# A spectral layer and a gated feed-forward on one core: the scheduler's other timing model

## The chip, the cores and the metric

One core of a Trainium2 chip runs the whole program. The metric is the device time of one execution in microseconds (us). The kernel before took 2654.95, 2657.49 and 2660.61 us in three runs; the median is 2657.49 us.

Five engines work side by side, each through its own instructions in a fixed order: PE (TensorE, matmuls; its weight loads are shown apart as PEld), DVE (VectorE), ACT (ScalarE), POOL (GpSimd) and SP (SyncE), which here issues the DMAs. An instruction that has to wait holds up everything behind it on its engine.

## The reference

For each of 8 batches, x has 3008 rows of 256 columns. The first half is a filter in the frequency domain, the second a feed-forward with a gate over all 24064 rows:

```python
X = np.fft.rfft(x, axis=1)
Yr = Xr @ w_r - Xi @ w_i + b_r          # Yi likewise
Y  = shrink(Yr, 0.01) + 1j * shrink(Yi, 0.01)
y  = np.fft.irfft(Y, n=3008, axis=1)
h  = y.reshape(24064, 256) @ w_in       # 256 x 2048
g  = h * np.clip(h + 3.0, 0.0, 6.0) / 6.0
out = g @ w_out                         # 2048 x 256
```

`shrink` moves each value towards 0 by 0.01 and stops at 0. `w_in` and `w_out` come in double precision.

## The kernel before

**The filter.** 3008 is 64 times 47, so each transform is done as two short ones, by matmuls with constant tables. Per batch there are three stages with DRAM scratch between them. `stage1` (line 496) loads x (`xin`), adds and subtracts mirrored halves (lines 520 and 521, on POOL from batch 2 on), multiplies by the 47-point table and stores `a`. `middle` (line 595) loads `bt`, does the 64-point transform (`s2`), the products with the weights and the shrinking (`s3`; `X` and `tc` are its tiles), and the way back (`s4`, `s5`). `segment` (line 697) loads `qt` and makes the rows of y in `raw`, a tile of 512 rows.

**The feed-forward.** The 24064 rows are 47 chunks of 512, and the 2048 inner columns 8 blocks of 256, so there are 376 units. `prepare` (line 793) makes seven operands `yb` of a chunk from `raw` by sums and differences, since the product with `w_in` is done by a scheme of seven half-size products in place of eight. A unit goes through `phase_a` to `phase_d` (lines 829 to 856): matmuls add up in the PSUM tiles `pb`, `pc` and `pd`; between them ACT copies an intermediate sum out of `pb` (`p`, `u`; line 824, and `h`, line 855) and DVE adds it to `pc` or `pd` into `h` (line 827). The next product that adds up in `pc` has to wait for that DVE add. There are two buffers of `pb`, and one each of `pc` and `pd`. `gate` (line 858) makes `r` and then `gs` of `h`: ACT line 862, DVE line 864, ACT line 131, DVE line 132. `down` (line 869) multiplies `gs` by `w_out` into `po`, in four calls a unit.

**Precision.** Each operand is split into a high and a low part (`split`, line 129), and `product` (line 134) does three matmuls where one would do: low by high, high by low, high by high. The three are called a triple below.

**The order in the code.** One loop (line 974) writes the units down as in a pipeline: in turn i stand `phase_a` of unit i, `phase_c`, `phase_d` and the start of the gate of unit i-1, `phase_b` of unit i, the rest of the gate of unit i-2, and the four `down` calls of unit i-3, one between each two phases. The stages of the filter are generators that are laid into quarter-turn slots (`lay`, line 920): a segment, for one, begins 8.5 units before its first row is used.

**The order that runs.** The framework's scheduler does not keep the order of the code. When the `TileContext` (line 1036) closes, it plays the program against a timing model of the machine: when an engine can take an instruction, it gets the one that stands first in the code among those whose inputs and buffers the model counts as there. What comes out is a fixed list of instructions for each engine, with the semaphores that it needs. Two helpers add edges by hand: `in_order` (line 174) ties every instruction of the start (the first batch's filter up to the first two chunks' operands) to the one before it on its engine, and `behind` (line 186) puts the last pieces of weight preparation after that start. From the first unit on, nothing else is tied.

## Time and profile before

| | |
|---|---|
| time, median of three | 2657.49 us |
| profiled execution, its own time | 2661.04 us |
| span of that execution in the trace | 2659.2 us |
| PE busy | 2586.7 us (97%), 16502 matmuls |
| DVE busy | 1962.6 us (74%) |
| ACT busy | 1816.4 us (68%) |
| POOL busy | 770.2 us (29%) |
| mean granted TensorE clock | 0.990 |

Busy time is the time in which an engine has an instruction in work; matmuls overlap, so that their steps (from start to start) are shorter than their durations.

### The profile page before, as it was taken

The page shows a single profiled execution, that of the slowest core. Times are in us where ns is not written, and L with a number is a line of the kernel's source. Part 1 is how long each engine was busy: PE and PEld are TensorE (multiplying, and loading weights), DVE is VectorE, ACT ScalarE, POOL GpSimd, SP SyncE. Part 2 cuts the span into 40 slices and gives each one's busy share as a digit, 9 for nine tenths or more (in the row PEclk, how much of TensorE's full clock was granted, in tenths as well). Part 3 has the DMA queues.
Part 4 walks back from the last instruction along what each step waited for, and adds up shares of the span by engine and source line. Part 5 has one row for each costly group of instructions (what it writes and reads, how often), then busy time and mean ns, then how long its engine had stood idle before and what let it go on. Part 6 is the DMA issues. An engine that isn't in the chain of part 4 may idle for free.

```text
span 2659.2 us, 44438 instructions
## 1 busy us (share of the span) xinstructions
PE 2586.7 (97%) x16502; PEld 2312.8 (87%) x16502; DVE 1962.6 (74%) x3175; ACT 1816.4 (68%) x3578; POOL 770.2 (29%) x739
## 2 busy tenths in 40 slices
PE   8789999999999999999999999999999999999999
PEld 5678889888888888888998988898899999999987
DVE  5877867777777777777777777777777777766666
ACT  3566767666766676676776777677676667666766
POOL 2253333332322332323323333323321122121210
PEclk9899999999999999999999999999999999999999
DMA  7524432222122221232212222222212111100000
GB/s 224 161 78 115 135 98 73 82 87 68 56 82 80 78 71 52 81 94 73 73 55 87 81 80 62 77 75 72 85 55 66 58 53 57 40 25 30 19 17 16
DMA packets 146096, 197.46 MB, mean 74 GB/s; under 512 B 16224, under 2 KB 101080, under 8 KB 145880
## 3 DMA queue, kind: packets, MB, share of 16 engines
q1 hardware_dynamic: 145879, 194.64, 25.0%
q8 instruction: 129, 2.11, 0.3%
q14 instruction: 88, 0.71, 0.1%
HBM read 97.58 MB, written 74.97 MB: 65 GB/s over the span
## 4 chain that ended last, share of the span: by engine, by line
PE 65%; DVE 10%; ACT 7%; issue 3%; POOL 1%; DMA 1%; ACTq 0%; SPq 0%; DVEq 0%; POOLq 0%
PE po L138 28%; PE pb L138 14%; PE pc L138 8%; PE ps_a L138 8%; PE pd L138 4%; ACT r L862 3%; DVE r L864 3%; PE ps_a L725 2%; DVE gs L132 2%; ACT gs L131 2%; PE ps_a L614 2%; DVE h L827 1%; DVE X L132 1%; DVE tc L655 1%; DMA xin<-in_x 0%
## 5 line engine op out<-in xcount | busy, mean ns | idle before, releaser
L138 PE MATMUL po<-gs,w_out_hi 128*128 128x512 f32 x3008 | 951.4, 397 | 1.8 <-DVE gs L132 1.8
L864 DVE SCALAR_TENSOR_TENSOR r<-r,h 128x1024 f32<-128x1024 f32 x376 | 478.0, 1271 | 381.8 <-ACT r L862 381.6
L138 PEld LDWEIGHTS po<-gs,w_out_hi 128*128 128x128 f32 x3008 | 565.7, 189 | 75.0 <-DVE gs L132 3.5
L138 PE MATMUL po<-gs,w_out_lo 128*128 128x512 f32 x1504 | 608.3, 405 | 2.3 <-ACT gs L131 2.3
L138 PE MATMUL pb<-yb,w_in_hi 128*128 128x256 f32 x3008 | 601.8, 282 | 0.0
L132 DVE TENSOR_TENSOR gs<-r,gs 128x1024 fp32r<-128x1024 f32 x376 | 476.4, 1267 | 124.8 <-ACT gs L131 122.0
L862 ACT ACTIVATE r<-h,three 128x1024 f32<-128x1024 f32 x376 | 433.3, 1152 | 192.5 <-DVE h L827 189.7
L138 PEld LDWEIGHTS pb<-yb,w_in_hi 128*128 128x128 f32 x3008 | 464.1, 190 | 50.4
L131 ACT CAST gs<-r 128x1024 fp32r<-128x1024 f32 x376 | 395.9, 1053 | 135.6 <-DVE r L864 122.7
L132 POOL TENSOR_TENSOR yb<-T,yb 128x256 fp32r<-128x256 f32 x184 | 204.9, 1124 | 815.1 <-ACT yb L131 815.0
L138 PE MATMUL pb<-yb,w_in_lo 128*128 128x256 f32 x1504 | 426.9, 284 | 8.8 <-ACT h L855 5.6
L827 DVE TENSOR_TENSOR h<-pc,u 128x256 f32<-128x256 f32 x752 | 313.9, 417 | 64.6 <-PE pc L138 60.5
L824 ACT COPY u<-pb 128x256 f32<-128x256 f32 x752 | 276.8, 371 | 104.0 <-PE pb L138 96.2
L138 PEld LDWEIGHTS pb<-yb,w_in_lo 128*128 128x128 f32 x1504 | 284.6, 189 | 67.3 <-ACT h L855 6.8
L138 PE MATMUL pc<-yb,w_in_hi 128*128 128x256 f32 x1504 | 299.6, 280 | 0.0
L138 PEld LDWEIGHTS po<-gs,w_out_lo 128*128 128x128 f32 x1504 | 284.1, 189 | 11.8 <-ACT gs L131 1.8
L138 PE MATMUL pc<-yb,w_in_lo 128*128 128x256 f32 x752 | 217.3, 289 | 23.3 <-DVE h L827 22.5
L855 ACT COPY h<-pb 128x256 f32<-128x256 f32 x376 | 140.0, 372 | 140.4 <-PE pb L138 139.1
L138 PEld LDWEIGHTS pc<-yb,w_in_hi 128*128 128x128 f32 x1504 | 231.5, 189 | 0.7
L138 PEld LDWEIGHTS pc<-yb,w_in_lo 128*128 128x128 f32 x752 | 142.4, 189 | 38.1 <-DVE h L827 36.3
L132 POOL TENSOR_TENSOR xs<-xin,xs 120x512 fp32r<-120x512 f32 (+1 forms) x49 | 65.5, 1336 | 344.3 <-ACT xs L131 271.5
L827 DVE TENSOR_TENSOR h<-pd,p 128x256 f32<-128x256 f32 x376 | 156.6, 416 | 3.9 <-ACT p L824 3.4
(150 smaller groups left out, 3940.4 us busy)
## 6 DMA issues: line engine op xcount, KB each, us to landing
bt<-scr SPq DMA_DIRECT2D x96, 256.0 KB, 3.0
scr<-pt SPq DMA_DIRECT2D x96, 256.0 KB, 2.0
out<-ot SPq DMA_DIRECT2D x94, 256.0 KB, 2.0
xin<-in_x SPq DMA_DIRECT2D x48, 480.0 KB, 4.6
scr<-a SPq DMA_DIRECT2D x96, 240.0 KB, 2.5
qt<-scr SPq DMA_DIRECT2D x96, 240.0 KB, 3.4
zt<-tc SPq DMA_DIRECT2D x336, 64.0 KB, 2.0
f<-in_f SPq DMA_DIRECT2D x96, 128.0 KB, 2.9
```

The source lines that it names most:

```text
L131: nc.scalar.copy(out=hi, in_=src)
L132: (on or nc.vector).tensor_tensor(out=lo, in0=src, in1=hi.bitcast(F32), op=ALU.subtract)
L138: nc.tensor.matmul(out=ps, lhsT=a, rhs=b, start=start and n == 0, stop=stop and n == len(todo) - 1, skip_group_check=more,)
L614: nc.tensor.matmul(out=psv[:, dh, :, u, :], lhsT=data[:, u, dh * P : (dh + 1) * P], rhs=f[:, u, :], start=True, stop=True,)
L655: nc.vector.tensor_tensor(out=t, in0=t, in1=c, op=ALU.subtract)
L725: nc.tensor.matmul(out=ps[:, cs * w + g * rows : cs * w + (g + 1) * rows], lhsT=qt[:rows, cs, g, dh * P : (dh + 1) * P], rhs=f47_s[2][:row ...
L824: nc.scalar.copy(out=t, in_=ps)
L827: nc.vector.tensor_tensor(out=hs[i][:, u, half * H : (half + 1) * H], in0=ps, in1=keep.pop((i, n)), op=ALU.add)
L855: nc.scalar.copy(out=hs[i][:, 1, :H], in_=pb)
L862: nc.scalar.activation(out=r, in_=h, func=AF.Relu, bias=three, scale=1.0)
L864: nc.vector.scalar_tensor_tensor(out=r, in0=r, scalar=6.0, in1=h, op0=ALU.min, op1=ALU.mult)
```

## The change

One argument is added where the context is made:

```diff
@@ -1033,7 +1033,7 @@
     for k in ("w_in", "w_out"):
         args[k] = args[k].bitcast(I32)
-    with tile.TileContext(nc) as tc:
+    with tile.TileContext(nc, schedule_with_timeline_sim=True) as tc:
         spectral_ffn(tc, **args)
```

The scheduler then plays the same program against its other timing model, which follows each instruction through its engine's sequencer, queue and datapath. The rule by which it picks, the code, the hand-made edges, the numbers of buffers and each instruction's shape stay as they are. What can differ is the order of instructions on each engine and of SP's DMAs, and with it the semaphores and which of a tile's buffers is used.

## Rows read from the trace of the kernel before

**Rows 1.** The page: PE and DVE busy time, share of the span and instructions, and the shares of the span by engine in the chain that ended last.

```profile
PE 2586.7 (97%) x16502; PEld 2312.8 (87%) x16502; DVE 1962.6 (74%) x3175; ACT 1816.4 (68%) x3578; POOL 770.2 (29%) x739
...
PE 65%; DVE 10%; ACT 7%; issue 3%; POOL 1%; DMA 1%; ACTq 0%; SPq 0%; DVEq 0%; POOLq 0%
```

**Rows 2.** The windows view: a stretch, its length, then busy time and number of instructions of PE, PEld, DVE, ACT and POOL, the granted TensorE clock, the share of DMA time and GB/s.

```profile
120.00:200.00 80.00, 66.03 (x353) 56.93 (x353) 65.06 (x105) 51.68 (x109) 38.16 (x32) 0.88 0.27 72
200.00:400.00 200.00, 190.51 (x1198) 170.24 (x1197) 147.91 (x231) 135.32 (x275) 68.61 (x64) 0.97 0.40 115
400.00:2300.00 1900.00, 1880.28 (x12175) 1695.87 (x12174) 1423.17 (x2325) 1330.65 (x2624) 569.94 (x525) 1.00 0.25 71
2300.00:2600.00 300.00, 300.00 (x1907) 270.42 (x1906) 207.03 (x326) 208.90 (x395) 61.99 (x72) 1.00 0.08 25
2600.00:2659.20 59.20, 53.55 (x315) 46.09 (x314) 35.76 (x50) 34.65 (x59) 3.06 (x3) 0.99 0.05 18
...
190.00:200.00 10.00, 7.27 (x31) 6.42 (x30) 7.00 (x11) 4.68 (x9) 3.92 (x3) 0.71 0.43 119
```

**Rows 3.** The timeline of PE in one unit near the end, where no stage of the filter is left: start, duration, what, tile written and tiles read. The lo rows are the first matmul of a triple.

```profile
2504.41 0.28 PE L138 MATMUL pc<-yb,w_in_lo 128*128 128x256 f32 x1
...
2504.76 0.39 PE L138 MATMUL po<-gs,w_out_lo 128*128 128x512 f32 x1
...
2505.45 0.28 PE L138 MATMUL pb<-yb,w_in_lo 128*128 128x256 f32 x1
...
2505.81 0.40 PE L138 MATMUL po<-gs,w_out_lo 128*128 128x512 f32 x1
...
2506.51 0.28 PE L138 MATMUL pb<-yb,w_in_lo 128*128 128x256 f32 x1
...
2506.87 0.28 PE L138 MATMUL pc<-yb,w_in_lo 128*128 128x256 f32 x1
...
2507.22 0.40 PE L138 MATMUL po<-gs,w_out_lo 128*128 128x512 f32 x1
...
2509.68 0.28 PE L138 MATMUL pc<-yb,w_in_lo 128*128 128x256 f32 x1
```

**Rows 4.** The timeline of DVE beside it. In brackets: idle time before, and what ended it.

```profile
2503.85 1.23 DVE L864 SCALAR_TENSOR_TENSOR r<-r,h 128x1024 f32<-128x1024 f32 x1 [1.28 <-ACT r L862]
2504.99 0.42 DVE L827 TENSOR_TENSOR h<-pd,p 128x256 f32<-128x256 f32 x1
2505.33 0.41 DVE L827 TENSOR_TENSOR h<-pc,u 128x256 f32<-128x256 f32 x1
2506.20 1.23 DVE L132 TENSOR_TENSOR gs<-r,gs 128x1024 fp32r<-128x1024 f32 x1 [0.46 <-ACT gs L131]
2507.43 0.42 DVE L827 TENSOR_TENSOR h<-pc,u 128x256 f32<-128x256 f32 x1
```

**Rows 5.** Waits of PEld and PE in 200 to 2300 us (who for whom: us in total, times, longest), and, from the view of line 827, how many of its adds there are and how long one takes (ns, least/median/most).

```profile
PEld pc L138 <- DVE h L827: 29.8, 46, 2.0
...
PE pc L138 <- DVE h L827: 17.0, 25, 1.5
...
L827 DVE TENSOR_TENSOR h<-pc,u x752: 406/417/426, 131.2 to 2647.5; 128x256 f32<-128x256 f32 x188
```

**Rows 6.** The timeline of one of the longest of these waits, DVE, POOL and PE, and (last) the operation of its third row at another time.

```profile
1158.57 1.95 DVE L132 TENSOR_TENSOR gs<-r,gs 128x1024 fp32r<-128x1024 f32 x1
...
1159.51 2.13 POOL L521 TENSOR_TENSOR xin<-xin 120x512 f32<-120x512 f32 x1
...
1160.44 1.48 DVE L132 TENSOR_TENSOR X<-xi,X 128x256 fp32r<-128x256 f32 x1
...
1161.84 0.41 DVE L827 TENSOR_TENSOR h<-pc,u 128x256 f32<-128x256 f32 x1
1162.31 0.39 PE L138 MATMUL pc<-yb,w_in_lo 128*128 128x256 f32 x1 [1.54 <-DVE h L827]
...
1211.79 0.42 DVE L132 TENSOR_TENSOR X<-xi,X 128x256 fp32r<-128x256 f32 x1
```

**Rows 7.** The timeline of a wait soon after the start, and of PE's `po` matmuls at 140 us.

```profile
140.41 1.20 PE L138 MATMUL po<-gs,w_out_hi 128*128 128x512 f32 x4
...
191.97 0.69 DVE L520 TENSOR_TENSOR e<-xin 120x512 f32<-120x512 f32 x1 [3.45 <-DMA xin<-in_x]
192.58 1.22 DVE L864 SCALAR_TENSOR_TENSOR r<-r,h 128x1024 f32<-128x1024 f32 x1
...
194.05 0.41 DVE L827 TENSOR_TENSOR h<-pc,u 128x256 f32<-128x256 f32 x1
194.52 0.58 PE L138 MATMUL pc<-yb,w_in_lo 128*128 128x256 f32 x1 [2.73 <-DVE h L827]
```

**Rows 8.** Waits over the whole span (who for whom: us in total, times, longest us), and two DMA issues (count, KB each, median us to landing).

```profile
POOL e L520 <- DMA xin<-in_x: 144.5, 40, 6.7
...
PE ps_a L725 <- DMA qt<-scr: 7.8, 2, 7.6
...
xin<-in_x SPq DMA_DIRECT2D x48, 480.0 KB, 4.6
...
qt<-scr SPq DMA_DIRECT2D x96, 240.0 KB, 3.4
```

## The prediction

> **What bounds the kernel now.** I read the page first: PE is busy for 97% of the span and holds 65% of the chain that ended last; DVE is at 74%, ACT at 68% [rows 1]. So time can come only from stretches in which PE waits, and the windows view says where those are [rows 2]. From 2300 to 2600 us, where nothing but the feed-forward is left, PE is busy for 300.00 of 300 us: it has no gap at all. From 400 to 2300 us it lacks 1900 - 1880.28 = 19.7 us, that is 1.0%. From 200 to 400 us it lacks 9.5 us and from 120 to 200 us 14.0 us, where the clock is also granted at a mean of 0.88 (0.71 from 190 to 200 us, so some of that stretch ran at 1.2 GHz in place of 2.4). After the start, then, a perfect order could win back 19.7 + 9.5 + 14.0 = 43 us, and a little clock; before 120 us the hand-made edges fix the order under either model. That is 43 us to gain and no such limit on what can be lost.
>
> Next I asked what PE waits for. In 200 to 2300 us it is nearly always one thing: the add of line 827 that must read `pc` before the next triple goes into it, 46 times and 29.8 us at the weight load, 25 times and 17.0 us at the matmul behind it [rows 5]. There are 752 such adds (two a unit), so about one in sixteen comes too late.
>
> Third, the unit near the end shows how much room an add has [rows 3, 4]. A `pc` triple runs from 2504.41 to 2504.76; the add that reads it ends at 2505.33 + 0.41 = 2505.74, and the `pc` matmul can follow some 0.06 us later (1161.84 + 0.41 = 1162.25 against 1162.31 [rows 6]). So PE needs 2505.80 - 2504.76 = 1.04 us of other work. It has a `po` triple (2504.76 to 2505.45, 0.69 us), a `pb` triple (0.36), another `po` triple (0.70) and another `pb` triple (0.36) before the next `pc` triple at 2506.87: 2.11 us of cover for 1.04 of need. The unit's period is 2509.68 - 2504.41 = 5.27 us, all of it PE's own steps.
>
> **The change part by part.** Nothing is removed or added: the same 16502 matmuls, 3175 DVE instructions and so on, at the same durations. What moves is the order on PE, DVE, ACT, POOL and SP from about 120 us on. I take the parts in turn.
>
> The start (to 120 us): 0, since every instruction is tied to the one before it on its engine. It has no cover to lose. Whether some untied instruction slips in between is bounded by one DVE operation, 1.2 us.
>
> The `down` calls on PE. The code puts one `po` triple between each two phases, and in the trace near the end PE keeps that order exactly [rows 3]. But a unit's four `po` triples wait for the same thing, `gs`; once it is written, all twelve matmuls can go. The scheduler does take them in a run when its model says so: at 140.41 us four of their hi matmuls stand together [rows 7]. A model that follows each engine's queue can hand PE an instruction before the array is free for it, so I expect it to give PE work nearer to the order in which it becomes ready, which bunches `po` triples. Price: with both `po` triples gone from behind a `pc` triple, the cover is two `pb` triples, 0.72 us, and 1.04 - 0.72 = 0.32 us of PE are exposed once a unit. With one gone it is 1.41 us, and nothing is exposed; the other half of the turn (2506.87 to 2509.68) has three short triples besides and stays covered. The ends are 0 (order as now) and 376 x 0.32 = 120 us (in each unit). Between them I take one unit in three, 125 x 0.32 = 40 us: the filter's own matmuls, laid between the phases until 2300 us, cover many units, so I stay nearer to the end that the trace shows now than to the other.
>
> The adds on DVE. `r` and `gs` take 1.23 us each [rows 4]. With its 2.11 us of cover an add can lie behind one of them and still come in time (1.04 + 1.23 = 2.27, 0.16 late); behind one that is drawn out, or behind two, it exposes more: 1.54 us in the instance of [rows 6]. The mean now is 29.8 / 46 = 0.65 us. The ends are all 29.8 us gone and every eighth of the 752 adds late in place of every sixteenth (94 x 0.65 = 61, so +31). I take 0: each model's list puts some adds behind such an operation and others not, and I see no row that makes one better at it.
>
> In the instance of [rows 6] DVE's `X` operation takes 1.48 us where it takes 0.42 at another time; it began while POOL's line 521 ran (1159.51 to 1161.64) and ended 0.28 us after that. The Trainium skill (SBUF — State Buffer, Who interferes with whom) says that a DVE instruction with two SBUF inputs and a GpSimd instruction that reads SBUF exclude each other, the later one waiting to the other's end. The rows agree with it here. By that rule how much DVE is drawn out depends on how much POOL and DVE work there is, not on the order, and a better order would not rid PE of its waits: it makes the rival "same" below likelier and leaves the sum as it is.
>
> DVE behind a DMA. At 191.97 us DVE sat 3.45 us on a load of `xin`, with the operation `r` and the `pc` add queued behind it; PE then waited 2.73 us [rows 7]. Here a model that knows that such a load lands after 4.6 us [rows 8] would put the adds first. The stretch from 120 to 400 us lacks 23.5 us in all; from 0 to a third of that (8 us) may come back, and the same may be lost in the transition. I take 0, with 8 us on either side for the range.
>
> POOL and SP. POOL waits 144.5 us for `xin`, up to 6.7 at a time [rows 8], and nobody waits for POOL to any length: it is 29% busy. A segment begins 8.5 units (8.5 x 5.27 = 45 us) before use, which covers a load of 3.4 us many times over. Cost 0 while that lead holds; without it, the third rival.
>
> Sum, against the profiled execution's own time: 2661.0 + 40 = 2701 us. That execution stands 3.5 us above the median of the runs, so the forecast is 2697.5 us, 1.5% slower. Its own range is from one unit in ten exposed (12 us, 2669) to all of them (120 us, 2778).
>
> **The rivals.** *Faster.* The other model's durations lie nearer to the chip's, so that the adds come to DVE ahead of the long operations, and DVE isn't parked on a DMA. For it: the waits are of one kind [rows 5], and [rows 7] shows an order made for a load that lands too soon. Against it: all there is to win is 43 us, and PE loses nothing in the stretch that has feed-forward alone. It decides where an add ends within its cover of PE work after the `pc` triple; if a third to a half of the 43 us comes back, the time is 2657.5 - 14 to 2657.5 - 22, 2636 to 2643 us.
>
> *Same.* Either the lists come out nearly alike, since PE is almost never short of the instruction that stands first in the code (from 2300 us on it runs exactly that order), or the change does nothing at all, or the waits move without becoming fewer, as in the instance with POOL. Within 5 us of 2657.5.
>
> *The filter comes late.* With work handed out as it becomes ready, the filter's chain of loads and stores for the next batch no longer keeps its slots; SP's queue is one list, and a load that waits for its buffer holds up the others. PE then stands still at the seam between batches, as it does at 104 us for `qt`, 7.6 us [rows 8]. For it: the stages are timed by slots that only order ties to the units. Against it: 45 us of lead. At two such waits in each of the seven later batches it is 7 x 2 x 7.6 = 106 us, 2764 us.
>
> **How the numbers follow.** Forecast (bunched `po`, exposed `pc` adds) 0.42; the filter late 0.10; faster 0.30; same 0.18. About 0.2%, 5 us, is what a measurement of this kernel can tell from no change. That gives faster 0.30, same 0.18, slower 0.52. The range runs from 2634, below which I leave some 0.08 of the faster case (more than half of the 43 us), to 2800, above which lie some 0.08 of the two slower ones (every unit exposed and adds late besides). Since it holds cases of both signs, the forecast's own range, 2669 to 2778, is the one to compare with if the sign is right.
>
> **What would show it.** If the forecast holds, PE's timeline from 2300 to 2600 us shows `po` triples in a row, PE is busy for less than 300 us there, and the waits of `pc` on line 827 are at least twice 46. If the faster rival holds, those waits shrink and 120 to 400 us lacks less than 23.5 us. If `qt`, `bt` or `yb` stand among PE's waits after 200 us, it is the third. The forecast is wrong if PE keeps the interleaving of the code in the last stretch: then its 40 us have no source.

## The result, and the profile after

The changed kernel takes 2672.37 us (median of five runs, 2670.17 to 2673.49) against 2658.41 us for the kernel before in the same five rounds: a ratio of 1.0056, with a 95% interval of 1.0045 to 1.0066. It is slower by 14 us. The forecast said slower, by 1.5%; it is 0.56%. The sign was right, the size was less than half of what was forecast, and one of the three rows that were to show the cause, the waits of `pc`, came out the other way.

The page of the changed kernel, which answers to [rows 1]:

```profile
PE 2604.8 (98%) x16502; PEld 2316.8 (87%) x16502; DVE 1966.9 (74%) x3175; ACT 1801.9 (67%) x3578; POOL 784.0 (29%) x739
...
PE 76%; DVE 4%; ACT 2%; issue 1%; DMA 0%; POOL 0%; SPq 0%; ACTq 0%; DVEq 0%
```

Read by themselves these lines look like an improvement: PE is busier, and it holds 76% of the chain where it held 65%. But the matmuls are the same 16502, and PE is busy 18 us longer with them: a matmul can last longer because it waits (below, 0.33 us for one that otherwise takes 0.28), and that counts as busy. The windows view, which answers to [rows 2], shows what that hides, if one reads the counts in brackets beside the busy time:

```profile
120.00:200.00 80.00, 71.82 (x403) 61.14 (x403) 67.07 (x113) 59.16 (x124) 46.92 (x37) 0.94 0.34 95
200.00:400.00 200.00, 190.95 (x1204) 169.91 (x1203) 147.54 (x229) 133.75 (x272) 70.36 (x60) 0.98 0.36 101
400.00:2300.00 1900.00, 1885.28 (x12147) 1695.68 (x12147) 1425.53 (x2327) 1316.16 (x2618) 568.06 (x526) 1.00 0.25 72
2300.00:2600.00 300.00, 298.24 (x1848) 263.77 (x1847) 202.17 (x311) 199.77 (x383) 65.59 (x67) 1.00 0.07 23
```

From 120 to 200 us PE does 403 matmuls where it did 353: this first part of the transition out of the start got faster. From 400 to 2300 us it is busy 5 us longer than before and does 28 matmuls fewer. From 2300 to 2600 us it is busy for all but 1.8 us and does 59 fewer (1848 for 1907). At 300 / 1907 = 0.157 us a matmul that is 9.3 us lost in the one stretch that had no gap at all before.

To place the losses exactly I took, from the trace, every step of PE from one matmul's start to the next and summed what it takes beyond the usual step of its size (0.234 us for 512 columns, 0.118 for 256, 0.111 for 128). This is my own sum, not a view; it holds every wait of PE, however short, and what a lower clock costs. The third row is an experiment that is told below. In us:

| stretch (us) | 0-120 | 120-200 | 200-400 | 400-2300 | from 2300 | all |
|---|---|---|---|---|---|---|
| before | 47.7 | 26.4 | 18.2 | 35.5 | 2.5 | 130.3 |
| after | 48.0 | 17.5 | 17.5 | 41.0 | 16.5 | 140.5 |
| timeline model, PE in code order | 49.0 | 21.7 | 21.7 | 22.3 | 6.4 | 121.1 |

After minus before is 10.2 us, which is the difference of the two spans (2669.5 - 2659.2 = 10.3), not that of the medians, 14. Each row is a single execution, and that of the kernel before lost more than others of its kind from 120 to 400 us. Four kernels of the experiments below (the four whose `down` calls are bunched by hand) have its lists on PE, DVE, ACT and POOL, operation by operation, up to 1000 us; they have 37.9 to 40.1 us there, not 44.6. From 200 to 400 us one of them does 1240 matmuls at a granted clock of 1.00, the kernel before 1198 at 0.97:

```profile
200.00:400.00 200.00, 190.75 (x1240) 170.91 (x1238) 151.65 (x241) 139.92 (x285) 74.17 (x67) 1.00 0.41 116
```

A second execution with the lists of the change has 35.8 where the first has 35.0. So the transition won some 4 us, not 9.6; the body lost 5.5 and the last stretch 14, and these add up to 15.

The same steps, split by the tile that the late matmul writes, say where the time is lost ("others" are `pd` and the filter's `ps_a`; a sum under 0 means steps a little shorter than usual):

| | `pc` | `po` | `pb` | others | all |
|---|---|---|---|---|---|
| 400-2300 us: before | 27.1 | -1.5 | 5.0 | 4.8 | 35.5 |
| after | 7.7 | 19.7 | 9.1 | 4.6 | 41.0 |
| timeline model, PE in code order | 13.5 | 0.5 | 2.8 | 5.5 | 22.3 |
| from 2300 us: before | 0.0 | 2.3 | 0.2 | 0.0 | 2.5 |
| after | 1.8 | 10.5 | 3.2 | 1.1 | 16.5 |
| timeline model, PE in code order | 0.2 | 5.7 | 0.4 | 0.1 | 6.4 |

From 400 us on the change wins 17.6 us at `pc` and loses 29.4 at `po` and 7.0 at `pb`.

The waits say the same. Of PE and PEld from 200 to 2300 us, answering to [rows 5] (who for whom: us in total, times, longest):

```profile
PEld po L138 <- DVE gs L132: 15.0, 26, 1.4
PEld pb L138 <- ACT u L824: 8.0, 21, 1.2
PEld pc L138 <- DVE h L827: 5.9, 14, 0.8
PEld po L138 <- ACT gs L131: 5.3, 16, 0.9
...
PE po L138 <- DVE gs L132: 9.2, 15, 1.2
PE ps_a L614 <- DMA bt<-scr: 3.0, 1, 3.0
...
PE pc L138 <- DVE h L827: 1.5, 4, 0.6
```

The wait that I had priced, `pc` for its add, shrank from 46 times and 29.8 us to 14 times and 5.9 us. In its place `po` waits for the `gs` that it multiplies. Before, this pair did not stand among the first seven of either list.

A unit near the end, PE and DVE together, answering to [rows 3, 4]:

```profile
2499.62 1.23 DVE L864 SCALAR_TENSOR_TENSOR r<-r,h 128x1024 f32<-128x1024 f32 x1 [1.28 <-ACT r L862]
...
2500.87 0.28 PE L138 MATMUL pc<-yb,w_in_lo 128*128 128x256 f32 x1
...
2501.42 0.42 DVE L827 TENSOR_TENSOR h<-pc,u 128x256 f32<-128x256 f32 x1 [0.57 <-PE pc L138]
...
2501.95 0.33 PE L138 MATMUL pc<-yb,w_in_lo 128*128 128x256 f32 x1
...
2502.42 1.23 DVE L132 TENSOR_TENSOR gs<-r,gs 128x1024 fp32r<-128x1024 f32 x1 [0.24 <-ACT gs L131]
...
2502.72 0.63 PE L138 MATMUL po<-gs,w_out_lo 128*128 128x512 f32 x2
...
2503.31 0.40 PE L138 MATMUL pb<-yb,w_in_hi 128*128 128x256 f32 x2
2503.56 0.42 DVE L827 TENSOR_TENSOR h<-pc,u 128x256 f32<-128x256 f32 x1
2503.70 0.76 PEld L138 LDWEIGHTS po<-gs,w_out_hi 128*128 128x128 f32 x4 [0.20 <-DVE gs L132]
2503.70 1.20 PE L138 MATMUL po<-gs,w_out_hi 128*128 128x512 f32 x4
...
2504.74 0.39 PE L138 MATMUL po<-gs,w_out_lo 128*128 128x512 f32 x1
...
2505.45 0.39 PE L138 MATMUL po<-gs,w_out_lo 128*128 128x512 f32 x1
...
2506.51 0.28 PE L138 MATMUL pc<-yb,w_in_lo 128*128 128x256 f32 x1
```

The four `po` triples no longer stand between the phases. Two lo matmuls go first, since they need only the high half of `gs` that ACT makes; then come four hi matmuls, then the other two triples, ten in one run. Counting such runs over the trace, nearly all were of three before (1102 of 1142 from 400 to 2300 us); after, they are of two and of ten (269 and 233). The unit takes 2506.51 - 2500.87 = 5.64 us where it took 5.27; it is one that loses more than the mean (14 us over the 67 units of this stretch, 0.21 each). Two things are to be seen. First, the next `pc` triple follows 1.08 us after the first with only two `pb` triples between, and still hardly waits: its add found DVE idle and began 0.20 us after the triple's end (2501.22). Second, the four hi matmuls at 2503.70 could have gone at 2503.31 + 2 x 0.118 = 2503.55, but DVE's `gs` ends only at 2502.42 + 1.23 = 2503.65.

### The profile page after: what moved, and what is told of

It is laid out like the page before. It is cut to its first block, busy times and chain, and to the rows that moved or that the text cites. A ratio compares the mean times of both kernels' runs of the same rounds, so it can differ in the third digit from the quotient of the medians.

```text
span 2669.5 us, 44497 instructions
## 1 busy us (share of the span) xinstructions
PE 2604.8 (98%) x16502; PEld 2316.8 (87%) x16502; DVE 1966.9 (74%) x3175; ACT 1801.9 (67%) x3578; POOL 784.0 (29%) x739
## 4 chain that ended last, share of the span: by engine, by line
PE 76%; DVE 4%; ACT 2%; issue 1%; DMA 0%; POOL 0%; SPq 0%; ACTq 0%; DVEq 0%
PE po L138 34%; PE pb L138 16%; PE ps_a L138 9%; PE pc L138 8%; PE pd L138 4%; PE ps_a L725 3%; PE ps_a L614 2%; DVE gs L132 2%; DVE r L864 1%; DVE h L827 1%; ACT r L862 1%; ACT gs L131 1%; DMA xin<-in_x 0%; DVE X L132 0%; DMA qt<-scr 0%
## 5 line engine op out<-in xcount | busy, mean ns | idle before, releaser
L138 PE MATMUL po<-gs,w_out_hi 128*128 128x512 f32 x3008 | 898.9, 399 | 12.5 <-DVE gs L132 11.4
L138 PEld LDWEIGHTS po<-gs,w_out_hi 128*128 128x128 f32 x3008 | 540.9, 189 | 124.4 <-DVE gs L132 22.2
L138 PE MATMUL pb<-yb,w_in_hi 128*128 128x256 f32 x3008 | 584.8, 281 | 1.7 <-DVE yb L132 1.7
L132 DVE TENSOR_TENSOR gs<-r,gs 128x1024 fp32r<-128x1024 f32 x376 | 489.4, 1302 | 82.0 <-ACT gs L131 80.1
L138 PE MATMUL po<-gs,w_out_lo 128*128 128x512 f32 x1504 | 540.3, 399 | 4.0 <-ACT gs L131 3.0
L132 POOL TENSOR_TENSOR yb<-T,yb 128x256 fp32r<-128x256 f32 x184 | 189.1, 1036 | 899.9 <-ACT yb L131 898.9
L138 PE MATMUL pb<-yb,w_in_lo 128*128 128x256 f32 x1504 | 435.2, 290 | 5.3 <-ACT u L824 2.7
L138 PEld LDWEIGHTS pb<-yb,w_in_lo 128*128 128x128 f32 x1504 | 283.4, 189 | 35.8 <-ACT u L824 10.2
L138 PEld LDWEIGHTS po<-gs,w_out_lo 128*128 128x128 f32 x1504 | 260.3, 189 | 46.6 <-ACT gs L131 9.1
L824 ACT COPY p<-pb 128x256 f32<-128x256 f32 x376 | 140.6, 374 | 73.9 <-PE pb L138 72.8
```

Of the source, the lines that this page charges most:

```text
L132: (on or nc.vector).tensor_tensor(out=lo, in0=src, in1=hi.bitcast(F32), op=ALU.subtract)
L138: nc.tensor.matmul(out=ps, lhsT=a, rhs=b, start=start and n == 0, stop=stop and n == len(todo) - 1, skip_group_check=more,)
L824: nc.scalar.copy(out=t, in_=ps)
```

## The experiments

Each was timed beside the kernel before in one of four sets of rounds, in which the medians of that kernel were 2655.96 to 2657.43 us; ratios are to it. All compute the whole output. The letters of theories hold within one group of runs. "Default" is the scheduler's model of the kernel before, "timeline" that of the change.

### Which engine's list costs the time

The first two tie all of PE's instructions from unit 0 on in the order of the code, under either model. The other engines' lists are what the scheduler makes beside it, and that is not what it made before: see below.

```diff
+    kept_in = [getattr(mybir.EngineType, e) for e in ("PE",)]
...
+    for ins in nc.cur_bb.bb.instructions[at[0] : None]:
+        if not type(ins).__name__.startswith("BassTile") and ins.engine in kept_in:
+            if ins.engine in before:
+                tc.add_manual_dep(ins, before[ins.engine].name, dep, reason="order")
+            before[ins.engine] = ins
...
-    with tile.TileContext(nc) as tc:
+    with tile.TileContext(nc, schedule_with_timeline_sim=True) as tc:
```

> The changed kernel (other timing model) with one thing undone: from the first unit on, PE's instructions are tied to the order of the code; DVE, ACT, POOL and SP are left to that model. Theory A (the loss is PE's new order: in the trace of the changed kernel po stands in runs of 2 and 10 matmuls in nearly every unit, where before it stood in runs of 3): the stretch without filter loses nothing again, the 14 us that it lost come back, and the gain of some 9 us before 200 us stays, since that is DVE's and ACT's order: about 2650 us, and the units near the end repeat every 5.27 us. Theory B (the loss comes from the new order on DVE and ACT, which makes gs and the copies late): 2670 us or more, with PE waiting for gs as in the changed kernel.

Measured: 2651.86 us (2650.04 to 2655.14), ratio 0.998 [0.9972, 0.9989]. With PE tied to the order of the code, the timeline model is 20.5 us faster than when it is free to order PE, and 0.2% faster than the kernel before; it is the fastest version of this study. Its rows in the tables above have the gain where the bunching had been: 18.7 us in the body and 10 from 2300 us on, most of it at `po`. From 120 to 400 us it has 43.4 where the change has 35.0; I had expected that stretch to stay.

One thing this run does not show: that PE's list alone did it. With PE tied, the scheduler made the other lists anew. To turn the change's lists into this kernel's, at least 1440 of DVE's 3175 instructions and 1792 of ACT's 3578 have to move; from the kernel before it is 397 and 452. So the loss belongs to PE's free order together with the lists made beside it. What bunching costs by itself is tried further down; the change's PE list beside other lists was not tried.

> The kernel before (default timing model) with PE tied to the order of the code from the first unit on: the control of the run beside it, with the very same list on PE. Both theories: within 5 us of the kernel before (2658 us), since PE follows the code in nearly every unit there already; if it is slower, PE's departures from the code around 120 to 400 us were worth that much.

Here the last changed line of the diff is left out. Measured: 2701.92 us, ratio 1.0166 [1.0153, 1.0179]. I had expected no more than 5 us; it is 44. And yet its lists differ little from the kernel before's: 255 of PE's 16502 matmuls, 124 of DVE's instructions and 159 of ACT's have to move. PE's list is the same as in the run before it, matmul for matmul, so the 50 us between these two are the other engines' lists. The waits of `pc` from 200 to 2300 us are 79.0 us here (PEld and PE together, a sum that counts one stall twice) and 22.1 there; the kernel before has 46.8. First the kernel of 2651.86 us, then that of 2701.92:

```profile
PE pc L138 <- DVE h L827: 8.3, 11, 1.9
...
PEld pc L138 <- DVE h L827: 13.8, 26, 2.1
```

```profile
PE pc L138 <- DVE h L827: 32.6, 50, 2.5
...
PEld pc L138 <- DVE h L827: 46.4, 63, 2.7
```

That led to the transplants: default model, PE in code order, and one engine's list, or two, tied in the order which the timeline model gave it in the run of 2651.86 us.

```diff
+    for engine, order in ORDERS.items():
+        mine = [
+            ins
+            for ins in nc.cur_bb.bb.instructions[at[0] :]
+            if not type(ins).__name__.startswith("BassTile") and ins.engine == getattr(mybir.EngineType, engine)
+        ]
+        if order:
+            moves = np.frombuffer(zlib.decompress(base64.b85decode(order)), "<i2")
+            mine = [mine[k + int(m)] for k, m in enumerate(moves)]
+        for one, next_one in zip(mine, mine[1:]):
+            tc.add_manual_dep(next_one, one.name, dep, reason="order")
```

The waits of 92.4 and 31 us that the next expectations give for 200 to 2300 us are those of the whole span; in the stretch named they are 79.0 and 22.1.

> Default model with TensorE in code order as in the run that took 2701.9 us, and in addition VectorE's instructions (3,029 of them, from unit 0 on) tied in the order that the timeline model gave them in the run of 2651.9 us. Theory D (the 50 us between these two runs is VectorE's list: filter operations ahead of the adds that pc waits for): 2650 to 2662 us, and the waits of pc for an add between 200 and 2300 us, 92.4 us in the kernel of 2701.9, fall to about 31. Theory A (it is ScalarE's list, with POOL's and SP's): 2692 to 2706 us, the waits stay. If the lists have to fit each other, something between, 2670 to 2690 us.

Measured: 2696.23 us, ratio 1.0143 [1.0128, 1.0158]: 6 of the 50 us. `pc` waits less (27.6 us at the weight load, 19.5 at the matmul), but PE now stands 20.4 us for `X` where it stood 8.8. The time is that of theory A, the waits are not: neither holds.

> Default model with TensorE in code order, and in addition ScalarE's instructions (3,459) tied in the order of the timeline model; the scheduler places VectorE's around them. Theory D: it stays at 2685 to 2705 us unless VectorE's list moves with ScalarE's. Theory A: 2650 to 2662 us, and pc's waits for an add between 200 and 2300 us fall from 92.4 to about 31 us.

Measured: 2681.98 us, ratio 1.0092 [1.0076, 1.0108]: 20 of the 50, and `pc` waits 29.1 and 21.7 us: the middle, which neither theory had. VectorE's list came part of the way by itself: 181 of its instructions stand otherwise than in the timeline model's list, 406 in the run of 2701.92.

> The reverse: timeline model with TensorE in code order, as in the run of 2651.9 us, but VectorE's instructions tied in the order that the default model gave them in the run of 2701.9 us. Theory D: 2692 to 2706 us, with pc waiting about 92 us for adds between 200 and 2300 us. Theory A: 2650 to 2662 us, waits near 31 us. If the lists have to fit each other, something between, 2670 to 2690 us.

Measured: 2807.81 us, ratio 1.0559 [1.0541, 1.0578], the slowest of all and 106 us slower than the kernel that VectorE's list was taken from. Theories D and A, and the middle, are all refuted. Its waits from 200 to 2300 us:

```profile
PE pc L138 <- DVE h L827: 91.4, 90, 4.0
...
PEld pc L138 <- DVE h L827: 113.6, 106, 4.2
```

> Default model with TensorE in code order, and both VectorE's and ScalarE's instructions tied in the order of the timeline model; only POOL's and SP's lists are the default model's. VectorE's list alone gave 2696.2 us, ScalarE's alone 2682.0, and the default's VectorE list among the timeline model's others 2807.8, so neither engine's list alone holds the 50 us. Theory F (a list is worth something only beside the lists that it was made with): 2650 to 2660 us, with pc's waits for an add between 200 and 2300 us near 31 us. Rival (POOL's and SP's lists, which the default model gave here too, hold what is left): 2675 to 2690 us, waits above 45 us.

Measured: 2657.48 us, ratio 0.9999 [0.999, 1.0009], and `pc` waits little:

```profile
PE pc L138 <- DVE h L827: 6.5, 9, 1.5
...
PEld pc L138 <- DVE h L827: 12.0, 26, 1.7
```

Tying VectorE's list is worth 6 us, ScalarE's 20, both together 44; here both are the timeline model's, instruction for instruction, and the body's excess is 21.2 us (59.0 without them). Tying VectorE's list from the other model costs 156 us (2807.81 - 2651.86). So a list's worth depends on the lists beside it. One reservation: where one list was tied, the scheduler filled the untied ones anew, so only the last of these four is close to a swap of two engines with all else kept.

A cause can be read from the traces. Of the late adds after 200 us (`pc` more than 0.06 us late), 28 stand right behind DVE's `X` in the run of 2701.92 us and cost PE 23.7 us, about half of the 50; in the runs of 2651.86 and 2657.48 none does.

### What bunching costs, alone

Here the default model stays, and from turn 309 on the code calls `down` four times right after `phase_a`. The scheduler may still spread them: 65 of 67 units have a run of eight to twelve `po` matmuls.

```diff
     for i in range(n + 3):
+        spread = not 309 <= i < 1000000
...
+        if not spread and 0 <= i - 3 < n:
+            for u in range(2):
+                for dh in range(2):
+                    down(i - 3, u, dh)
```

> The kernel before (default timing model) with one part of the new order done by hand: from unit 309 on the code writes a unit's four calls of down in one run, right after phase_a, in place of one between each two phases. Theory A with the price of the prediction, 0.32 us a unit: 67 x 0.32 = 21 us slower; with the price read from the changed kernel's last stretch, 14 / 67 = 0.21 us a unit: 14 us slower, about 2672 us. Theory B: within 5 us of the kernel before.

Measured: 2672.31 us, ratio 1.0056 [1.0043, 1.0068], by chance the time of the change. About 15 us over 67 units is 0.22 a unit, as expected from the change's last stretch. It is lost at other tiles, though: 4.2 us at `pc`, 5.7 at `po` and 5.4 at `pb`, where the change has 1.8, 8.2 and 3.0. The windows view from 2300 to 2600 us shows the mark of the change, PE busy and short of matmuls (1829; 1907 before, 1848 after):

```profile
2300.00:2600.00 300.00, 299.39 (x1829) 262.62 (x1828) 200.48 (x309) 199.58 (x377) 58.85 (x68) 1.00 0.07 25
```

The same in the middle of the body, turns 121 to 187, where the filter's matmuls lie between the phases:

> The kernel before (default model) with the run of e4 in units 121 to 187, some 67 units of the stretch that has filter work between the phases (about 1000 to 1470 us). Theory A with cover: the filter's matmuls stand between the phases and hide most of it; read from the changed kernel against e1 (41.0 - 22.3 = 19 us over some 280 units, 0.07 us a unit) it is 67 x 0.07 = 5 us. Rival: the run costs the same everywhere, 67 x 0.22 = 15 us.

Measured: 2662.98 us, ratio 1.0021 [1.0012, 1.003]: 6.4 us over 67 units, 0.095 a unit, less than half of what it costs in the last stretch. That fits matmuls of the filter that cover the rest; it was not shown in another way.

Next, the default model with bunched `down` calls from turn 325 on, and PE tied to that order, so that all twelve matmuls stand together; and the same with `gs` made a turn earlier than it is used.

> As e6a, but the run is of the unit three turns back, as in the code before, with two buffers of gs: the run of 12 alone, PE tied to the order of the code from unit 325 on. Both theories: 10 us or more over the kernel before (0.22 us a unit in e4; 51 units); if it is within 5 us, the cost in e4 was neither cover nor lead but the order that the scheduler made beside the run.

Measured: 2711.66 us, ratio 1.0205 [1.0191, 1.0219]: 55 us over 51 units, 1.08 a unit, where 10 to 16 us were expected. By tile, 45 of the 55 us are at `pc`. The waits of PEld from 2400 to 2650 us, and one unit's timeline:

```profile
PEld pc L138 <- DVE h L827: 31.0, 35, 0.9
```

```profile
2553.32 0.28 PE L138 MATMUL pc<-yb,w_in_lo 128*128 128x256 f32 x1
...
2554.16 1.23 DVE L132 TENSOR_TENSOR gs<-r,gs 128x1024 fp32r<-128x1024 f32 x1 [0.30 <-ACT gs L131]
2554.45 0.39 PE L138 MATMUL pb<-yb,w_in_lo 128*128 128x256 f32 x1 [0.26 <-ACT u L824]
...
2555.30 0.42 DVE L827 TENSOR_TENSOR h<-pc,u 128x256 f32<-128x256 f32 x1
2555.77 0.39 PE L138 MATMUL pc<-yb,w_in_lo 128*128 128x256 f32 x1 [0.69 <-DVE h L827]
```

This is the mechanism of the forecast, at twice its price: `pc`'s cover is two `pb` triples, the add stands behind `gs` (2554.16 + 1.23 = 2555.39), and PE waits 0.69 us for it where I had 0.32, besides 0.26 for ACT.

> The kernel before (default model); from unit 325 on a unit's four calls of down stand in one run as in e4, but of the unit one turn further back, so that gs is written a whole turn (5.3 us) ahead of its use; a third buffer of gs is made of the filter's idle buffers; PE is tied to the order of the code from there on, so that the runs stay 12 long. Beside it e6b without the extra turn. Theory of the prediction (the run takes away what covers the pc and pb copies): both cost alike, 51 units x 0.2 to 0.3 = 10 to 16 us over the kernel before. Theory L (the run stands right where gs is written, so PE has no lead over gs and pays for each little lateness): this one costs at most 4 us, and e6b 10 us or more.

```diff
+        if i > 325 and 0 <= i - 4 < n:
+            for u in range(2):
+                for dh in range(2):
+                    down(i - 4, u, dh)
```

Measured: 2706.32 us, ratio 1.0186 [1.0172, 1.02]; `pc` waits as often (36 times, 31.9 us at the weight load from 2400 to 2650). In a strict run of twelve the age of `gs` matters little: 5 us of 55, and the lateness at `po` falls from 3.9 us to nothing, while that at `pc` stays. Theory L is refuted here; in the change itself, whose runs are of two and ten, `po` is the main loss.

### Putting PE's order back in part

The change with PE tied to the code's order in the last stretch only (from unit 309), and from unit 33 on (about 400 us), so that the transition keeps its gain.

```diff
-    for ins in nc.cur_bb.bb.instructions[at[0] : None]:
+    for ins in nc.cur_bb.bb.instructions[at[309] : None]:
```

> The changed kernel with PE tied to the order of the code only from unit 309 on, the stretch after some 2300 us that has no filter work. Theory A: the 14 us that this stretch lost come back, the rest stays: 2672 - 14 = about 2658 us. Theory B: 2670 us or more.

Measured: 2663.07 us, ratio 1.002 [1.001, 1.003]: 9.3 us back of the 14 lost there; the steps of PE from 2300 us on exceed the usual by 6.5 us (16.5 after, 2.5 before).

> The changed kernel (other timing model) with PE tied to the order of the code from unit 33 on, that is from about 400 us; before that PE keeps the model's order. Counted in PE steps above their usual length, the changed kernel lost 35 us between 120 and 400 us and the kernel tied throughout (e1) 43 us, while from 400 us on they lost 57 and 29 us. Theory A (bunched po costs from 400 us on; in the transition PE's free order pays): both good halves add up, some 8 us under e1's 2652: about 2643 us. Rival: what the start of the list won is lost again when the tie begins, about 2652 us.

Measured: 2655.53 us, ratio 0.9999 [0.999, 1.0007], where 2643 was expected. Its sums over the five stretches are 48.1, 17.7, 27.3, 26.1 and 6.6 us: the transition's gain is there (17.7) and is lost again in the next stretch (27.3, where PE in code order throughout has 21.7 and the change 17.5). The rival's reason holds, and the trace says where: until 388 us PE's list is that of the change, and right behind the joint PE stands still for ACT and for a load of `qt`, 8 us together (in brackets, idle time before and what ended it). Why that load lands so late there was not tried:

```profile
391.85 0.65 PE L138 MATMUL ps_a<-z,g_lo 128*128 128x512 f32 x1 [2.19 <-ACT z L131]
...
402.00 1.18 PE L725 MATMUL ps_a<-f_all,qt 120*128 120x120 f32 x4 [5.94 <-DMA qt<-scr]
```

## Why the prediction was right and wrong

**The start: right.** 47.7 and 48.0 us of excess before 120 us.

**The `down` calls bunch on PE: right, and more than I had.** I took one unit in three; it is nearly every unit. That bunching costs time is shown by the kernels with calls bunched by hand under the default model (0.22 us a unit in the last stretch, where the change loses 14 / 67 = 0.21), and time comes back where PE is put back in code order under the timeline model, with the other lists made anew.

**The step that failed** is "with both `po` triples gone from behind a `pc` triple, the cover is two `pb` triples, 0.72 us, and 1.04 - 0.72 = 0.32 us of PE are exposed once a unit". The cover did shrink to two `pb` triples, but that wait did not grow: lateness at `pc` fell from 27.1 to 9.5 us from 400 us on, and in the last stretch it is 1.8 us over 67 units, 0.03 a unit. The loss stands at the next station, which I had not named: `po` takes `gs` as it comes off DVE, and the hi matmuls of a run wait for it, 0.15 us in the unit shown. That is 29.4 us at `po` and 7.0 at `pb`, against a gain of 17.6 at `pc`. So bunching was foreseen, the wait through which it costs was not, and that the sum came out slower at all, and by a third of the forecast, owes something to luck.

The price went wrong in one reading. I took PE's need of 1.04 us from a unit in which the add of `pc` stood behind an add of `pd`, which itself came after `r` [rows 4]: it began 2505.33 - 2504.76 = 0.57 us after the triple. Where DVE is idle the add begins 0.20 us after it, so 0.37 us of the 1.04 were DVE's queue, and the next `pc` matmul came 2501.95 - 2501.22 = 0.73 us after the triple, just the 0.72 of two `pb` triples. Hardly anything is left exposed at `pc`. It took the strict run of twelve, where the add queues behind `gs`, to bring the `pc` wait back.

**"The adds on DVE: I take 0" failed.** It was a gain: 19.4 us of lateness at `pc` in the body. Of the late adds after 200 us none stands behind `X` any more (15 did before, 9.7 us). With PE in code order the timeline model has 22.3 us of excess in the body where the kernel before has 35.5, and the transplants show that this gain sits in VectorE's and ScalarE's lists together. The change has other lists than that kernel, so its 19.4 us cannot be parted into what the lists of DVE and ACT gave and what the long `po` run gave, in which DVE can catch up. The idle time of DVE ahead of these adds does not part them either. From the grouped lines (busy us, mean ns, then DVE's idle time just before and what ended it), before, after, and timeline model with PE in code order:

```profile
L827 DVE TENSOR_TENSOR h<-pc,u 128x256 f32<-128x256 f32 x752 | 313.9, 417 | 64.6 <-PE pc L138 60.5
...
L827 DVE TENSOR_TENSOR h<-pc,u 128x256 f32<-128x256 f32 x752 | 314.9, 419 | 199.5 <-PE pc L138 191.1 <-ACT u L824 3.0 <-ACT gs L131 0.6
...
L827 DVE TENSOR_TENSOR h<-pc,u 128x256 f32<-128x256 f32 x752 | 313.4, 417 | 78.9 <-PE pc L138 70.7 <-ACT u L824 5.1
```

It trebles in the change, where DVE sits 0.57 us for PE in the unit shown, and hardly rises in the third kernel, which is the fastest.

**DVE behind a DMA: 0, with 8 us on either side: right within its bound.** The tables have 44.6 before and 35.0 after from 120 to 400 us, but against the four other executions of the same lists, 37.9 to 40.1, some 4 us came back. Whether the load of `xin` [rows 7] had a part in it was not tried.

**The rule on DVE and POOL.** I drew from it that how much DVE is drawn out hangs on the amount of work and not on the order. The Trainium skill (SBUF — State Buffer, Who interferes with whom) does not say that; it says "Issue order, not op shape, decides who blocks." The runs show that the order counts. DVE's 84 `X` operations, drawn out where POOL works beside them [rows 6], take 567 ns in the mean before and 584 after, but 644 in the timeline model with PE in code order:

```profile
L132 DVE TENSOR_TENSOR X<-xi,X 128x256 fp32r<-128x256 f32 x84 | 54.1, 644 | 6.0 <-ACT X L131 4.4
```

That kernel is the fastest all the same, so neither does it follow that PE would keep its waits: the drawn-out operations no longer stand ahead of an add.

**What was to show it.** "`po` triples in a row" and "PE busy for less than 300 us there" came true, the second by only 1.8 us. "The waits of `pc` at least twice 46" was wrong, 14. Both signs of the faster rival came true in a kernel that is slower: those waits shrank, and 120 to 400 us lacks 17.2 us of PE's time (before, 23.5). The rival with the filter late shows once, 3.0 us of `bt` at 200 to 400 us.

## What to carry to other kernels

When a scheduler's model is changed, compare the lists engine by engine and hold one at a time, PE's first: here the timeline model was 50 us better than the default when both were held to PE's code order, and 14 us worse when both were free, and the total alone showed neither. Then count what moved in the lists that were not held, since the scheduler makes them anew. Before a stretch of one trace is called faster, look for another execution of the same lists: here some 5 of 9.6 us were that one execution's own. A need of cover read from a unit in which the producer had to queue is an upper end, not a price; read it once more where the engine was idle. On an engine that is always busy, count the instructions in each window, since busy time can rise while work falls, as PE's did from 400 to 2300 us.

## What I had not expected of the hardware

A wait of PE that is too short for the view of waits still costs. From 2300 us on, steps that take 0.06 to 0.15 us too long number 63 after and 19 before, 6.2 us against 1.7, and another 27 against 1 lie between 0.15 and 0.30 us (5.4 us against 0.2). Together they are 9.7 of the 14 us lost there, and the view of waits of the weight loads in 2300 to 2600 us names only these for `po`:

```profile
PEld po L138 <- DVE gs L132: 2.8, 12, 0.3
...
PEld po L138 <- ACT gs L131: 0.7, 3, 0.2
```

And PE's own order says little without the others': the same list of 16502 matmuls took 2651.86, 2657.48, 2681.98, 2696.23, 2701.92 and 2807.81 us beside six sets of lists.
